# Fourier mixing and a gated convolution on one core: the odd columns of the odd samples computed as a DCT-IV

## The chip, the cores and the metric

The kernel runs on one core of one Trainium2 chip. A core has TensorE (PE, matmuls; its weight loads, PEld, are listed apart), VectorE (DVE), ScalarE (ACT), GpSimd (POOL) and SyncE (SP, which issues DMAs). The metric is the device time of one execution in microseconds (us); lower is better.

## The reference

Input x has 8 batches of 3136 x 256 numbers (float32). The first part is the real part of a two-dimensional Fourier transform of each batch; the second is a feed-forward layer whose hidden values are gated by a sigmoid of a convolution over the sequence with three taps.

```python
X = np.fft.fft(np.fft.fft(x, axis=1), axis=2).real       # per batch: sequence, then features
h = np.maximum(X @ w_in, 0.0)                             # 256 -> 1024
conv = sum(conv_w[k] * h_padded[:, k:k + S, :] for k in range(3))
out = (h * sigmoid(conv)) @ w_out                         # 1024 -> 256
```

The weights arrive as float64 and are narrowed to float32 in the kernel by integer operations on VectorE.

## The kernel before

The transform along the sequence uses the symmetries of cosine and sine. For each batch, `fold_ops` adds and subtracts rows of x and their mirror images on VectorE until a quarter of the sequence is left, and writes the result as the tile `w`: two of them, one for even and one for odd frequencies (`wt[b][0]`, `wt[b][1]`), each with 98 or 99 partitions, four parts, four groups of samples q and 128 features. A batch has two halves of the fold (`half(h)`), each an ordered list of seven operations, most of them an instruction of 1000 elements per partition or two of 500: `pair(0)`, `pair(2)`, `both(6)`, `feats(1)` (which writes the odd `w`), `both(4)`, `evens`, `feats(0)`. Beside them `single`, a small copy on GpSimd, fills the first column of each part of `w`.

`units` then multiplies `w` by tables of cosines and sines that a DMA has loaded into SBUF. There are eight units a batch (the ninth, `feature`, exists for batch 0 alone): for each of sn = 1 and 0 (sine and cosine) `odd_even`, `odd`, `even_even` and `even`. A unit is a few matmuls into one PSUM tile, then a copy of a part of it to SBUF on ScalarE (`copy`), then additions and subtractions on VectorE (`fin`). `odd` has four matmuls of HO = 392 columns, no copy, and two VectorE instructions of 392 elements that write the odd columns of `PQ` and their mirror image. One float32 matmul of the program appears in the profile as two instructions, each with a weight load. `tabs[0]` holds the even tables (two kinds, four sample groups, 393 columns), `tabs[1]` the odd ones (four kinds: two are loaded, and `mirror_tables` makes the other two on ScalarE).

The rest of the work is a list of 256 steps: 8 batches x 4 chunks of columns x 8 blocks of 128 hidden features. A step's parts are spread over several turns (cycles) of the last loop of the program. In cycle t:

- TensorE does `products` of step t+1 (`pb`, `pa`: two matmuls of some 387 columns, the second part of the transform and `w_in` in one) and then `mm2` of step t-3 (`po`, six matmuls of 256 columns with `w_out`);
- ScalarE does `sigmoid` of step t-2, `copies` of step t+1 (out of `pb`), `seed` of step t+2, `first_tap` of step t;
- VectorE does `combine` of step t (L719), `tap` 1 of step t-1 (L730), then what is hung into the cycle under the name "dve" (a fold operation or the `fin` of a unit), `tap` 2 of step t-1, and `gate` of step t-2 (L754);
- GpSimd does its share of the gate (L753) and issues the indirect loads of x.

Each engine works in the order of the program. Folds and units of later batches are hung into these cycles by hand: `ends` lists in which cycle the fold of each batch must be over (9, 20, 44, 68, 96, 125, 157, 189), and the units of that batch run from there to three cycles before its first step. `at(cycle, where, fn)` hangs an operation into a cycle: "act" stands after `copies` on ScalarE, "dve" between the two taps on VectorE, "pe" after `mm2` on TensorE. A cycle that is in `taken` gets no fold operation.

Batch 0 runs before the steps. VectorE folds both halves (from 8.7 us), then narrows the first quarter of `w_in`. TensorE meanwhile runs 16 instructions without use to keep its clock up (`keep_on`, which read the odd `w` of the first half), and then the parts of the four odd units in turn (`u.part(i)`). The tables are loaded on SP's queue behind the loads of x; the odd tables first, then a quarter of `w_in`, then the even ones.

Of the kernel before, what the change touches and what calls it, by code (L numbers as in the profile page):

```python
# [30 lines left out]
NQ = 8  # L31
# [5 lines left out]
def kernel(  # L37
# [103 lines left out]
    def fold_ops(b):  # L141
# [4 lines left out]
        def half(h):  # L146
# [60 lines left out]
        (o0, s0), (o1, s1) = half(0), half(1)  # L207
        return o0 + o1, {**s0, **{len(o0) + j: f for j, f in s1.items()}}

    tabs = [const.tile([P, n, HQ, HE], F32, name="tab%d" % n) for n in (2, 4)]
# [3 lines left out]
    def table(k, st, q, cols):  # L216
        return tabs[st // 2][0:k, st, q, cols] if st < 2 else tabs[1][0:k, st - 2, q, cols]

    def load_tables(par):


        st = slice(2 * par, 2 * par + 2)
        to = tabs[par][:, 0:2].rearrange("p s q i -> p s (q i)")
        n = HQ * HE
        m = NP // 2 // 16 * 16
        for i in range(2):
            nc.sync.dma_start(out=to[i:2 * m:2], in_=dft_seq[0:m, st, HQ * i:HQ * (i + 1)]
                              .rearrange("p s q i -> p s (q i)"))
        assert NP == 2 * m + 2
        nc.sync.dma_start(out=to[2 * m:NP], in_=bass.AP(  # L230
            tensor=dft_seq.tensor, offset=dft_seq.offset + (m * 4 + 2 * par) * NQ * HE,
            ap=[[n, 2], [NQ * HE, 2], [1, n]]))
        nc.sync.dma_start(out=to[NP:KR], in_=bass.AP(
            tensor=dft_seq.tensor, offset=dft_seq.offset + ((NP * 4 + 2 * par) * NQ - HQ + 2) * HE,
            ap=[[n, 1], [NQ * HE, 2], [1, n]]))

    def mend_row(par, half):

        for st in range(2):
            row = tabs[par][96:NP, st, HQ - 1]  # L240
            act(row, row, AF.Copy, scale=half[96:NP])

    def mirror_tables(q):

        for to, of, s in ((2, 1, -1.0), (3, 0, 1.0)):
            for i in range(2):
                act(tabs[1][0:KR, to, q:q + 2, i:HO:2], tabs[1][0:KR, of, q:q + 2, i:HO:2], AF.Copy,
                    scale=-s if i else s)
# [31 lines left out]
    def units(b):  # L280
# [52 lines left out]
        def odd(sn):  # L333
            prods = [(q, wf, st) for q in (0, 2) for wf, st in stat(sn)]
            mms = [product((slice(0, P), slice(0, HO)), wf, st, q, slice(0, HO), i == 0, i == 3)
                   for i, (q, wf, st) in enumerate(prods)]

            def fin(p):
                a, bb, t = a_[sn][:, 0:HO], p[:, 0:HO], PQ[b][sn]
                vt(t[:, 1:Q4 + 1:2], a, bb, op=ALU.add)  # L340
                x0, x1 = (bb, a) if sn else (a, bb)
                vt(t[:, M - 1:Q4:-2], x0, x1, op=ALU.subtract)
            return Unit(b, mms, lambda p: None, fin)
# [277 lines left out]

    nc.gpsimd.memset(tabs[1][0:1, 0, 0, 0:1], 0.0)
    load_tables(1)
    w_in[0].load(nc.sync)
    load_tables(0)
# [172 lines left out]
    for f in fold_ops(0)[0]:  # L798
        f()
# [6 lines left out]
    mirror_tables(0)  # L806
    mend_row(1, half)
    mirror_tables(2)
# [61 lines left out]
    ends = [9, 20, per + 12] + [per * (b - 1) - 3 + max(11 - 4 * (b - 2), 0) for b in range(3, B)]  # L870
# [37 lines left out]
    for b in range(1, B):  # L908
        ops, singles = fold_ops(b)
        c0, n = ends[b - 1], ends[b] - ends[b - 1]  # L910
        if b == 1:

            cs = [c for c in range(4, ends[1] + 1) if c not in taken]
            assert len(cs) == len(ops) and cs[7] > NF + 4
# [3 lines left out]
        if b + 1 < B:  # L918
            for h in range(2):
                for j, fn in enumerate(load_ops(b + 1, h, nc.sync)):  # L920
                    at(cs[7 * h + 6] + 1 + j, "load", fn)
# [112 lines left out]
```

## Time and profile before

| | |
|---|---|
| time, median of 3 runs | 1188.49 us (1187.96 to 1189.62) |
| span of the profiled execution (first to last instruction) | 1184.7 us; its whole time is not listed, and the runs lie 3.3 to 4.9 us above this span |
| PE busy | 1158.7 us (98%) |
| DVE busy | 1128.7 us (95%) |
| ACT busy | 886.7 us (75%) |
| POOL busy | 407.6 us (34%) |
| mean granted clock of TensorE | 0.998 |

A line of the timeline gives the start, the length, the engine, the line of the code, the instruction, what it writes and reads, its shape and how many of its kind follow each other; in brackets stand the idle time of the engine before it and what ended it. Lengths overlap: an instruction often starts before the one ahead of it on the same engine has ended, so what an engine can do in a time is read from start to start (the pitch). Groups of instructions give count, busy time in us and mean length in ns. Windows give the busy time of PE, PEld, DVE, ACT and POOL in a stretch.

### The profile page before, as it was taken

The page shows a single profiled execution, that of the slowest core. Times are in us where ns is not written, and L with a number is a line of the kernel's source. Part 1 is how long each engine was busy: PE and PEld are TensorE (multiplying, and loading weights), DVE is VectorE, ACT ScalarE, POOL GpSimd, SP SyncE. Part 2 cuts the span into 40 slices and gives each one's busy share as a digit, 9 for nine tenths or more (in the row PEclk, how much of TensorE's full clock was granted, in tenths as well). Part 3 has the DMA queues.
Part 4 walks back from the last instruction along what each step waited for, and adds up shares of the span by engine and source line. Part 5 has one row for each costly group of instructions (what it writes and reads, how often), then busy time and mean ns, then how long its engine had stood idle before and what let it go on. Part 6 is the DMA issues. An engine that isn't in the chain of part 4 may idle for free.

```text
span 1184.7 us, 15354 instructions
## 1 busy us (share of the span) xinstructions
PE 1158.7 (98%) x4820; PEld 891.6 (75%) x4820; DVE 1128.7 (95%) x1633; ACT 886.7 (75%) x1888; POOL 407.6 (34%) x476
## 2 busy tenths in 40 slices
PE   4999999999999999999999999999999999999998
PEld 2667777777777777777777777777777777777776
DVE  7899999999999999999998999999998898999996
ACT  2578668777777778877777877877777777888885
POOL 5225443433434342424333232432322232222222
PEclk9999999999999999999999999999999999999999
DMA  9803233121212021202131110310010100100000
GB/s 226 195 10 107 57 55 89 49 69 41 72 38 86 28 77 52 83 7 76 34 96 46 48 48 14 104 34 27 27 34 21 32 27 27 51 31 27 28 27 32
DMA packets 70068, 66.08 MB, mean 56 GB/s; under 512 B 28107, under 2 KB 57683, under 8 KB 69987
## 3 DMA queue, kind: packets, MB, share of 16 engines
q1 hardware_dynamic: 64349, 51.98, 15.6%
q0 software_dynamic: 5120, 12.85, 3.7%
q8 instruction: 38, 0.62, 0.2%
q14 instruction: 43, 0.35, 0.1%
q10 hardware_dynamic: 518, 0.28, 0.1%
HBM read 39.33 MB, written 25.74 MB: 55 GB/s over the span
## 4 chain that ended last, share of the span: by engine, by line
PE 89%; DVE 7%; issue 1%; POOL 1%; ACT 1%; DMA 0%; DVEq 0%; SPq 0%; POOLq 0%; ACTq 0%
PE po L92 54%; PE pb L92 14%; PE pa L92 13%; PE pd L92 8%; DVE g L730 3%; DVE h L719 1%; DVE g L754 1%; POOL xh L131 1%; DVE raw L558 0%; DVE xh L167 0%; DVE wout L551 0%; ACT os L778 0%; DVE w L194 0%; DVE win L551 0%; DMA out_dram<-os 0%
## 5 line engine op out<-in xcount | busy, mean ns | idle before, releaser
L92 PE MATMUL po<-wout,g 128*128 128x256 f32 x3072 | 706.1, 379 | 4.2 <-DVE g L754 4.2
L92 PEld LDWEIGHTS po<-wout,g 128*128 128x128 f32 x3072 | 580.8, 190 | 148.7 <-issue 20.0
L730 DVE SCALAR_TENSOR_TENSOR g<-h,cw,g 128x770 f32<-128x770 f32 (+1 forms) x512 | 575.7, 1124 | 5.7 <-ACT g L725 2.1
L753 POOL TENSOR_TENSOR g<-g,h 128x385 f32<-128x385 f32 (+2 forms) x256 | 270.4, 1057 | 721.1 <-ACT g L745 542.1
L708 ACT ACTIVATE nb<-pb 128x386 f32<-128x386 f32 (+2 forms) x494 | 219.9, 500 | 168.2 <-PE pb L92 167.5
L745 ACT ACTIVATE g<-g 128x385 f32<-128x385 f32 (+4 forms) x512 | 244.8, 531 | 81.8 <-DVE g L730 78.4
L719 DVE CUSTOM_DVE_ANT_0 h<-pa,nb 128x386 f32<-128x386 f32 (+2 forms) x503 | 260.0, 556 | 2.5 <-POOL h L686 2.5
L725 ACT ACTIVATE g<-h,cw 128x770 f32<-128x770 f32 (+1 forms) x256 | 244.2, 954 | 0.0
L92 PE MATMUL pb<-qt,G 127*128 127x387 f32 (+2 forms) x512 | 213.7, 498 | 0.9 <-ACT G L641 0.9
L92 PE MATMUL pa<-pt,G 128*128 128x387 f32 (+2 forms) x512 | 211.8, 494 | 0.0
L672 ACT ACTIVATE pa<-eb,ge 128x387 f32<-128x387 f32 (+2 forms) x256 | 155.2, 607 | 0.6 <-ACT ft L477 0.6
L92 PEld LDWEIGHTS pa<-pt,G 128*128 128x128 f32 x512 | 96.9, 189 | 73.5 <-issue 18.0
L754 DVE TENSOR_TENSOR g<-g,h 128x385 f32<-128x385 f32 (+2 forms) x256 | 147.7, 577 | 2.4 <-ACT g L745 2.4
L92 PE MATMUL pd<-tab,w 98*128 98x196 f32 (+3 forms) x448 | 115.9, 356 | 0.0
L92 PEld LDWEIGHTS pb<-qt,G 127*128 127x128 f32 x512 | 91.5, 190 | 18.8 <-ACT G L641 1.9
L131 POOL DMA_INDIRECT xh<-in_x_dram,idx x64 | 99.8, 1560 | 13.0 <-issue 10.6
L92 PEld LDWEIGHTS pd<-tab,w 98*128 98x128 f32 (+1 forms) x448 | 82.7, 191 | 12.6
L778 ACT COPY os<-po 128x256 f32<-128x256 f32 x196 | 57.6, 397 | 6.6 <-PE po L92 3.3
L156 DVE TENSOR_TENSOR xh<-xh 98x1020 f32<-98x1020 f32 (+1 forms) x32 | 40.4, 1265 | 2.6 <-DMA xh<-in_x_dram,idx 2.6
L167 DVE TENSOR_TENSOR xh<-xh 98x1024 f32<-98x1024 f32 (+1 forms) x32 | 40.5, 1266 | 0.1
L178 POOL COPY w<-xh 98x4 f32<-98x4 f32 (+1 forms) x32 | 24.2, 758 | 6.1 <-DVE xh L167 3.6
L193 DVE TENSOR_TENSOR w<-xh 98x508 f32<-98x508 f32 (+1 forms) x32 | 23.0, 720 | 0.1
(124 smaller groups left out, 330.3 us busy)
## 6 DMA issues: line engine op xcount, KB each, us to landing
out_dram<-os SPq DMA_DIRECT2D x192, 128.0 KB
xh<-in_x_dram SPq DMA_DIRECT2D x16, 784.0 KB
eb<-ed SPq DMA_DIRECT2D x16, 193.5 KB
tab<-dft_seq_dram SPq DMA_DIRECT2D x4, 589.5 KB
raw<-in_moe_w_in_dram SPq DMA_DIRECT2D x4, 512.0 KB
raw<-in_moe_w_out_dram SPq DMA_DIRECT2D x1, 2048.0 KB
eb<-ed SPq DMA_DIRECT2D x8, 209.0 KB
eb<-ed SPq DMA_DIRECT2D x7, 193.0 KB
```

The source lines that it names most:

```text
L92: nc.tensor.matmul(o, l, r, start=start, stop=stop, skip_group_check=True)
L131: nc.gpsimd.indirect_dma_start(out=xh[b, h][0:NP, 7 - m].rearrange("p q d -> p (q d)"), out_offset=None, in_=bass.AP(tensor=x.tensor, offs ...
L167: vt(flat(to, to + 2), flat(0, 2), flat(2, 4), op=op)
L672: act(pa[s][:, 0:n], eb[b, c], AF.Copy, scale=ge[:, f:f + 1])
L708: act(nb[s][:, i, cols], p[:, cols], AF.Copy, scale=-1.0 if i else 1.0)
L719: nc.vector._custom_dve(TENSOR_ADD_SAT, out=to, in0=a[:, cols], in1=c[:, i, cols], s0=BIG, s1=0.0)
L725: act(gs[s], hs[s][:, 0:n], AF.Copy, scale=cw[:, 0, s[2]:s[2] + 1])
L730: stt(out=g, in0=h[:, k:k + n], scalar=cw[:, k, f:f + 1], in1=g, op0=ALU.mult, op1=ALU.add)
L745: act(gs[s][:, c], gs[s][:, c], AF.Sigmoid)
L753: gt(g[:, p], g[:, p], h[:, p], op=ALU.mult)
L754: vt(g[:, v], g[:, v], h[:, v], op=ALU.mult)
L778: nc.scalar.copy(out=osb[:, j % 2], in_=pt[:, j % 2])
```

## The change

The odd samples (groups q = 0 and 2) at the odd frequencies form a transform in which both indices are odd (a DCT-IV, and the sine of the same kind). The new kernel turns each pair of values by an angle that depends on the sample alone, and can then use the even tables, at every second column, 197 instead of 392, for two of the turned parts in place of the odd tables; sums and differences of the two results give all odd columns. In detail:

- Fold: behind `both(4)` each half gets an eighth operation, `turned`: two `scalar_tensor_tensor` of 98 x 256 on VectorE, in place in the odd `w`. Ahead of it, in the same cycle under "act", `scaled` writes two products of 98 x 256 on ScalarE into a new tile `rt`. The angles are the tile `turn`, loaded by four DMAs of 98 single numbers each on ScalarE's queue at the start.
- `odd`: four matmuls of 197 columns in place of 392, a copy of 197 columns on ScalarE, and two more VectorE instructions of 196 elements ahead of the two of 392, whose operands are now both in SBUF.
- Tables: of the odd ones two sample groups and 196 columns are left. Eight small DMAs load them, then the even ones follow, and `w_in` behind both. The mirroring shrinks from eight instructions of 392 elements to four of 196.
- The fold of batch 1 must be over in cycle 22 instead of 20, so its units start two cycles later.

```diff
@@ fold_ops @@
-            ops = [pair(0), pair(2), both(6, ALU.subtract), feats(1), both(4, ALU.add), evens, feats(0)]
-            return ops, {3: single(1), 6: single(0)}
+            def sides():
+                w = wt[b][1][0:NP, :, 2 * h]
+                return w[:, 0:4:2], w[:, 1:4:2]
+            made = []
+            def scaled():
+                made.append(rp.tile([P, 2, 2, P], F32, name="rt", tag="rt"))
+                for i, v in enumerate(sides()):
+                    act(made[0][0:NP, i], v, AF.Copy, scale=turn[0:NP, 1, h:h + 1])
+            def turned():
+                for i, v in enumerate(sides()):
+                    stt(out=v, in0=v, scalar=turn[0:NP, 0, h:h + 1], in1=made[0][0:NP, 1 - i],
+                        op0=ALU.mult, op1=ALU.add if i else ALU.subtract)
+            ops = [pair(0), pair(2), both(6, ALU.subtract), feats(1), both(4, ALU.add), turned, evens, feats(0)]
+            return ops, {3: single(1), 7: single(0)}, {5: scaled}
...
+    def load_turn(eng):
+        for s in range(2):
+            for i in range(2):
+                eng.dma_start(out=turn[i:NP:2, s].unsqueeze(2), in_=bass.AP(
+                    tensor=dft_seq.tensor, offset=dft_seq.offset + ((2 + s) * NQ + HQ * i) * HE,
+                    ap=[[4 * NQ * HE, NP // 2], [2 * HE, 2], [1, 1]]))
...
@@ units: odd(sn) @@
-            prods = [(q, wf, st) for q in (0, 2) for wf, st in stat(sn)]
-            mms = [product((slice(0, P), slice(0, HO)), wf, st, q, slice(0, HO), i == 0, i == 3)
-                   for i, (q, wf, st) in enumerate(prods)]
+            n = HE // 2 + 1
+            mms = [product((slice(0, P), slice(i * n, (i + 1) * n)), w(4 + 2 * sn + (i ^ sn)), i, q,
+                           slice(0, HE, 2), i == 0 and q == 0, q == 2)
+                   for q in (0, 2) for i in range(2)]
+            def copy(p):
+                a_["s", sn], a_["b", sn] = [asp.tile([P, HO + 2], F32, name="as", tag="as") for _ in range(2)]
+                nc.scalar.copy(out=a_["s", sn][:, 0:n], in_=p[:, n:2 * n])
             def fin(p):
-                a, bb, t = a_[sn][:, 0:HO], p[:, 0:HO], PQ[b][sn]
+                a, t = a_[sn][:, 0:HO], PQ[b][sn]
+                u, v, bb = p[:, 0:n], a_["s", sn][:, 0:n], a_["b", sn][:, 0:HO]
+                if sn:
+                    vt(bb[:, 0:HO:2], v[:, 0:n - 1], u[:, 0:n - 1], op=ALU.add)
+                    vt(bb[:, 1:HO:2], v[:, 1:n], u[:, 1:n], op=ALU.subtract)
+                else:
+                    vt(bb[:, 0:HO:2], u[:, 0:n - 1], v[:, 0:n - 1], op=ALU.subtract)
+                    vt(bb[:, 1:HO:2], u[:, 1:n], v[:, 1:n], op=ALU.add)
                 vt(t[:, 1:Q4 + 1:2], a, bb, op=ALU.add)
                 x0, x1 = (bb, a) if sn else (a, bb)
                 vt(t[:, M - 1:Q4:-2], x0, x1, op=ALU.subtract)
-            return Unit(b, mms, lambda p: None, fin)
+            return Unit(b, mms, copy, fin)
...
@@ start @@
+    load_turn(nc.scalar)
     nc.gpsimd.memset(tabs[1][0:1, 0, 0, 0:1], 0.0)
-    load_tables(1)
+    load_odd(nc.sync)
+    load_even()
     w_in[0].load(nc.sync)
-    load_tables(0)
...
@@ order of the side work @@
-    ends = [9, 20, per + 12] + [per * (b - 1) - 3 + max(11 - 4 * (b - 2), 0) for b in range(3, B)]
+    ends = [9, 22, per + 12] + [per * (b - 1) - 3 + max(11 - 4 * (b - 2), 0) for b in range(3, B)]
...
+        for j, fn in pres.items():
+            at(cs[j], "act", fn)
```

More of the change, by code (lines that the diff above doesn't have):

```diff
@@ L237, in mend_row @@
+    def load_turn(eng):
+        for s in range(2):
+            for i in range(2):
+                eng.dma_start(out=turn[i:NP:2, s].unsqueeze(2), in_=bass.AP(
+                    tensor=dft_seq.tensor, offset=dft_seq.offset + ((2 + s) * NQ + HQ * i) * HE,
+                    ap=[[4 * NQ * HE, NP // 2], [2 * HE, 2], [1, 1]]))
     def mend_row(par, half):
         for st in range(2):
-            row = tabs[par][96:NP, st, HQ - 1]
+            row = tabs[0][96:NP, st, HQ - 1] if par == 0 else tabs[1][96:NP, st, 1]
@@ L797 @@
     nc.gpsimd.memset(PQ[0][1][96:P, :], 0.0)
-    for f in fold_ops(0)[0]:
+    ops, _, pres = fold_ops(0)
+    for j, f in enumerate(ops):
+        if j in pres:
+            pres[j]()
         f()
```

54 lines of the change are left out of this document (34 added, 20 removed).

## The prediction

> **What bounds the kernel now.** I read the busy times, then the chain of waits, then a quiet cycle of the timeline, then windows.
>
> ```profile
> PE 1158.7 (98%) x4820; PEld 891.6 (75%) x4820; DVE 1128.7 (95%) x1633; ACT 886.7 (75%) x1888; POOL 407.6 (34%) x476
> ...
> PE 89%; DVE 7%; issue 1%; POOL 1%; ACT 1%; DMA 0%; DVEq 0%; SPq 0%; POOLq 0%; ACTq 0%
> ```
>
> By the shares both TensorE and VectorE look full; the chain that ended last is 89% TensorE. A quiet cycle late in the run (nothing hung in) tells them apart:
>
> ```profile
> 1067.35 0.87 POOL L753 TENSOR_TENSOR g<-g,h 128x385 f32<-128x385 f32 x1 [2.98 <-ACT g L745]
> 1067.51 2.57 DVE L730 SCALAR_TENSOR_TENSOR g<-h,cw,g 128x770 f32<-128x770 f32 x2
> 1067.69 0.81 PE L92 MATMUL pb<-qt,G 127*128 127x386 f32 x2
> 1068.34 0.81 PE L92 MATMUL pa<-pt,G 128*128 128x386 f32 x2
> 1068.54 0.87 ACT L708 ACTIVATE nb<-pb 128x385 f32<-128x385 f32 x2 [0.86 <-PE pb L92]
> 1068.99 2.75 PE L92 MATMUL po<-wout,g 128*128 128x256 f32 x12
> 1070.00 0.55 DVE L754 TENSOR_TENSOR g<-g,h 128x385 f32<-128x385 f32 x1
> 1071.58 0.82 PE L92 MATMUL pb<-qt,G 127*128 127x387 f32 x2
> ```
>
> TensorE's matmuls follow each other without a gap: 3.89 us from `pb` to `pb` (1067.69 to 1071.58), 2.59 of it for twelve `po`. ScalarE waits 0.86 us for it. VectorE's two taps take 2.49 us (1067.51 to 1070.00) while GpSimd's gate runs inside them. In another cycle the same instructions need less:
>
> ```profile
> 951.06 2.06 DVE L730 SCALAR_TENSOR_TENSOR g<-h,cw,g 128x770 f32<-128x770 f32 x2
> 953.04 0.56 DVE L754 TENSOR_TENSOR g<-g,h 128x385 f32<-128x385 f32 x1
> 953.51 1.02 DVE L719 CUSTOM_DVE_ANT_0 h<-pa,nb 128x386 f32<-128x386 f32 x2
> 954.45 1.01 DVE L730 SCALAR_TENSOR_TENSOR g<-h,cw,g 128x770 f32<-128x770 f32 x1
> ```
>
> From tap to tap: 3.39 us, the taps 1.98. So VectorE's own work in a cycle is 0.50 us below TensorE's, and the busy share hides it: it is stretched when it is early. TensorE is the bound where this holds, and VectorE where it does not:
>
> ```profile
> 80.00:100.00 20.00, 19.09 (x76) 13.95 (x75) 19.93 (x27) 14.46 (x29) 9.79 (x9) 1.00 0.17 51
> 200.00:250.00 50.00, 49.40 (x205) 36.67 (x205) 49.32 (x73) 39.57 (x88) 21.28 (x27) 1.00 0.16 50
> 550.00:600.00 50.00, 50.00 (x209) 38.39 (x208) 49.03 (x74) 38.13 (x78) 19.00 (x18) 1.00 0.10 31
> ...
> PEld po L92 <- DVE g L754: 15.6, 24, 1.5
> 220.27 2.86 PE L92 MATMUL po<-wout,g 128*128 128x256 f32 x12 [0.37 <-DVE g L754]
> ```
>
> Up to some 120 us, and again around 200 to 260 us, TensorE loses time to VectorE's gate (windows of 19.09 of 20 and 49.40 of 50; the wait of 0.37 at 220.27); from 550 on it loses none.
>
> **TensorE's gain.** In batch 1 whole units stand in one cycle:
>
> ```profile
> 141.04 2.80 PE L92 MATMUL pd<-tab,w 98*128 98x392 f32 x8
> 143.68 0.81 PE L92 MATMUL pb<-qt,G 127*128 127x387 f32 x2
> 156.38 1.56 PE L92 MATMUL pd<-tab,w 98*128 98x197 f32 x8
> 157.78 0.87 PE L92 MATMUL pb<-qt,G 127*128 127x418 f32 x2
> 25.72 8.10 PE L92 MATMUL po<-tab,w 98*128 98x196 f32 x32
> ```
>
> Eight instructions of 392 columns take 2.64 us (0.33 each), eight of 197 from the same strided even table 1.40 (0.175). An odd unit saves 1.24; with two a batch that is 2.48, and 17.4 for batches 1 to 7. In batch 0 the 16 of 392 among the 32 at 25.72 save 2.5. The new form is in the trace, so this term is nearly certain as work.
>
> **VectorE's cost.** The rows nearest to each added instruction:
>
> ```profile
> 948.18 0.36 DVE L298 TENSOR_TENSOR as<-as,pd 128x197 f32<-128x197 f32 x1 [1.99 <-ACT as L294]
> 948.45 0.36 DVE L300 TENSOR_TENSOR as<-pd,as 128x196 f32<-128x196 f32 x1
> 948.73 1.01 DVE L730 SCALAR_TENSOR_TENSOR g<-h,cw,g 128x770 f32<-128x770 f32 x1
> 930.33 0.55 DVE L340 TENSOR_TENSOR qt<-as,pd 128x392 f32<-128x392 f32 x1
> 930.80 0.55 DVE L342 TENSOR_TENSOR qt<-pd,as 128x392 f32<-128x392 f32 x1
> L558 DVE SCALAR_TENSOR_TENSOR raw<-raw 128x512 f32<-128x512 uint32 x3 | 2.1, 693 | 0.1
> L641 ACT COPY G<-po 128x256 f32<-128x256 f32 x8 | 2.7, 372 | 3.3 <-PE po L92 3.3
> ```
>
> An odd `fin` gets two additions of 196, 0.27 us each by pitch, and a wait of 0.1 for their result (taps that depend on each other take 1.98 where two single ones would take 1.87, estimated from the lengths): 0.65 a unit, 1.3 a batch. `turned` is four instructions of 256 elements a batch. They lie between 0.27 (the 196 above) and 0.61 (0.69 long for 512, less the 0.08 by which lengths overlap); I take 0.33, as 256 is much nearer to 196: 1.3 a batch. Together 2.6; by the ends 2.4 and 3.7. ScalarE gets four products of 256 (0.37 at most each, by L641) and two copies of 197, some 2.1 a batch; it is busy 75% and waits for `pb` in every quiet cycle, so I cost it at nothing except where VectorE waits for it.
>
> Does VectorE have 2.6 us? In a batch the quiet cycles leave 32 x 0.50 = 16; the units add some 12.4 of TensorE (16 x 0.33, and 48 of the smaller forms at 0.10 to 0.175), folds and `fin`s some 22.4 of VectorE (a fold operation of 1000 elements has a pitch of 1.14, an estimate from a length of 1.2; eight such, four of 0.6, eight of 0.6; `fin`s of 6.0, eight instructions of 0.27 and eight of 0.47). That leaves 6, some 8 with the longer last chunks, in which TensorE has more room still. The change takes 2.6 on one side and 2.5 on the other, so about 3 remain: TensorE stays first over a batch, with VectorE ahead in more places.
>
> The row at 948.18 shows a new kind of wait: VectorE stood 1.99 us until ScalarE had copied a part of the product. `odd` had no copy; now it has, and `turned` waits for `scaled` in the same way, four such places a batch. Behind each in VectorE's queue stand tap 2 and the gate that `po` needs. In a cycle that begins with `pb` at 0, ScalarE starts `copies` at 0.85 (1067.69 to 1068.54), ends them at 1.64 and the new copy near 2.0; the longer `fin` ends at 3.6, tap 2 at 4.55, the gate at 5.1. The next `po` starts at 3.89 + 1.30 = 5.2, later where a unit's matmuls lie between (0.3 to 0.6). It fits, barely: I take 0 and keep 0.5 for each of 28 as the other end.
>
> [...]
>
> [...]
>
> **The start.** In front of the first step VectorE, GpSimd and TensorE hang together:
>
> ```profile
> 13.66 1.22 DVE L167 TENSOR_TENSOR xh<-xh 98x1024 f32<-98x1024 f32 x1
> 14.91 0.69 DVE L171 TENSOR_TENSOR xh<-xh 98x512 f32<-98x512 f32 x1
> 15.63 0.64 POOL L199 TENSOR_TENSOR w<-xh,sg 98x4 f32<-98x4 f32 x1
> 15.71 4.64 PE L92 MATMUL pb<-w 98*128 98x512 f32 x5 [8.87 <-POOL w L178]
> 29.44 0.69 DVE L561 SCALAR_TENSOR_TENSOR win<-raw,win 128x512 f32<-128x512 f32 x1
> 32.55 0.36 DVE L328 TENSOR_TENSOR as<-as,po 128x196 f32<-128x196 f32 x1 [2.42 <-ACT as L324]
> 45.52 11.67 SPq L436 DMA_DIRECT2D ft<-in_x_dram  x3
> ```
>
> `turned` stands where L171 started at 14.91. It needs `scaled`, and that needs the columns that GpSimd writes until 16.27 (15.63 + 0.64): two products make it 17.0. VectorE stands 2.1 us, then works 0.7; the second half costs 0.7 without a stall. `keep_on` reads the turned `w`, so TensorE's row at 15.71 moves to about 17.7, and the odd parts from 25.72 to 27.7; with the 2.5 saved they end no later. VectorE is 3.5 late at 30.1; the 2.42 us it waited before 32.55 absorb that much; the longer `fin`s add 1.3, a shorter wait later gives back 0.4: some +2.0. Up to 120 us VectorE sets the pace, so this reaches the steps.
>
> The DMAs: `turn` has 392 single numbers. The three gathers at 45.52 (3136 numbers each) hold their queue 3.9 us each, so by that rate these take 0.5; between that and four plain issues they are there long before 16.3, and loads of the odd tables, though eight, carry a quarter of the bytes. ScalarE's queue holds nothing urgent then. The first quarter of `w_in` now lands behind the even tables (by the tiles' sizes 1.2 MB of even tables more ahead of it, and 0.9 MB of odd ones less), and VectorE asks for it 3.5 us later too. `scaled` of the second half stands ahead of the mirroring on ScalarE, to some 26 us; the mirrored tables are first read by the second round of odd parts, at some 29, and mirroring has shrunk to a quarter. I cost all this at 0; if one landed only at 20 us, 3 us more.
>
> **Up to 260 us.** To the 2.0 VectorE adds batch 1's turn (1.3) and `fin`s (1.3) and batch 2's turn (1.3): 5.9 by the end of the second fold, where it sets the pace. Batch 1's units also stand closer (9 cycles instead of 11). Against it stand VectorE's idle time (0.7 in 200:250, some 2.5 over 120 to 260 us) and stretched taps, perhaps 1: I take +2.5 at 260 us, and batch 1's saving of 2.48 is gone in it. Ends: 0 and +6.
>
> **The sum.** From batch 2 on six batches save 2.48 each: -14.9. In the stretches between the units of one batch and the next, where only folds run, VectorE is ahead for a few cycles; that costs +1.5 in all (0 to 4). -14.9 + 2.5 + 1.5 = -10.9. The span goes from 1184.7 to 1174; the runs lie 3.8 above it at the median, so 1188.5 becomes 1177.6; I say 1178.
>
> **Rivals.**
> - All of the saving comes through: the start is absorbed and VectorE follows, -17.4 and 0 for the start: 1171. For it: the new matmul form is in the trace and 550:600 has no gap. Against it: the waits at 220.27 and before.
> - VectorE is the bound at its busy share. 49.03 of 50 leaves 1 us in 50, 2.8 in a batch, if the stretch is not elastic but belongs to the work. Then 2.6 of new work uses it up, a batch takes what it took, and the start (+2.0 to +2.5) remains: 1191. It decides from 2.8 us of added VectorE time a batch, which any contention with GpSimd passes. Against it: the cycle at 951.06, and that a quiet cycle shows VectorE full with 3.39 of work.
> - The new waits for ScalarE's copies reach `po`: 0.2 us for 28 of them, 5.6 more than I forecast: 1183 to 1184.
> - The change does not do what it says, if matmuls of 197 were paced by their weight loads; the row at 156.38 (0.175) excludes it.
>
> **Chances.** The forecast (1174 to 1181) 0.45; all comes through 0.15; ScalarE's waits 0.20; VectorE the bound, or something like it in the start, 0.20. Changes within 0.2% (2.4 us) can hardly be measured. Faster: the first three, 0.78 with a little taken off the third; same 0.05; slower 0.17. The range, 1171 to 1191, leaves out the tails of the first and last cases.
>
> **What would show it.** Right: 16-instruction groups of 98x197 at 0.175 in the `pd` rows, TensorE without gaps from 300 us on, quiet-fold stretches with waits of `po` for the gate, PE busy some 18 to 20 us less, DVE busy up at most by a few, first steps some 2 us later. Wrong: waits of `po` on the gate in the 550:600 window, DVE at 50 of 50 with unstretched taps, or a first `po` much later than 63 us.

## The result and the profile after

The changed kernel takes 1195.62 us (median of four runs, 1194.77 to 1195.90) against 1188.22 us (1185.01 to 1189.62) for the kernel before on the same chip: ratio 1.0067, 95% interval 1.0053 to 1.0081. It is slower by 0.7%; I had said 1178. The span of the profiled execution went from 1184.7 to 1193.9 us.

The busy times and the shares of the chain of waits, after:

```profile
PE 1154.3 (97%) x4820; PEld 891.5 (75%) x4820; DVE 1135.4 (95%) x1697; ACT 898.3 (75%) x1932; POOL 403.3 (34%) x476
...
PE 74%; DVE 16%; issue 4%; ACT 3%; DMA 2%; POOL 1%; SPq 0%; DVEq 0%; POOLq 0%; ACTq 0%
```

TensorE is busy only 4.4 us less (1158.7 to 1154.3) where the change takes some 20 us of matmuls away (in e7_matmuls below, without VectorE's added work, it is 18.4 less: 1140.3); VectorE has 6.7 us more. On the chain TensorE's share fell from 89% to 74% and VectorE's rose from 7% to 16%. The same windows as before (columns: window, length, then busy time and count of PE, PEld, DVE, ACT, POOL, then granted clock, DMA share, GB/s), and a stretch around 365 us:

```profile
80.00:100.00 20.00, 18.25 (x71) 12.94 (x70) 19.86 (x31) 13.13 (x27) 5.11 (x13) 1.00 0.12 31
200.00:250.00 50.00, 48.06 (x196) 34.60 (x195) 49.15 (x73) 37.66 (x82) 20.78 (x27) 1.00 0.20 57
340.00:390.00 50.00, 48.49 (x194) 35.39 (x193) 48.88 (x73) 37.10 (x82) 21.16 (x27) 1.00 0.22 64
550.00:600.00 50.00, 49.78 (x215) 39.52 (x214) 49.76 (x76) 38.34 (x79) 23.85 (x20) 1.00 0.19 59
```

The waits after (what waits, for what; us in all, times, longest):

```profile
PEld po L92 <- DVE g L811: 48.5, 83, 1.8
...
PE po L92 <- DVE g L811: 10.2, 22, 1.2
```

TensorE is short of full in all four (before: 19.09 of 20, 49.40 of 50, 49.97 in 340:390 and 50.00 in 550:600), and its waits for the gate, 15.6 and 4.2 us before, are 48.5 and 10.2 (most of the first kind is a weight load that waits beside a running matmul). VectorE's new waits for ScalarE, in the groups of waits after (L217 is `turned`, L391 and L394 the first addition of an odd `fin`):

```profile
DVE w L217 <- ACT rt L213: 6.5, 12, 2.0
...
DVE as L394 <- ACT as L385: 3.1, 3, 1.7
...
DVE as L391 <- ACT as L385: 2.0, 4, 0.8
```

To see where the time went, I compare the start of each step's `po` matmuls in the two traces (worked out from the TensorE rows; step 41 starts at 252.3 us before, which ends the stretch that the prediction called "up to 260 us"):

| stretch | predicted | measured |
|---|---|---|
| start of the program to the first `po` (63.0 us before, 72.7 after) | +2.0 | +9.7 |
| first `po` to step 41 | +0.5 | +5.9 |
| step 41 to the last step | -13.4 | -6.5 |
| sum | -10.9 | +9.1 |

Differences in the text are taken before rounding. The profiled execution of the kernel before, which all of them are measured against, was itself a quick one: in every run listed core by core the time is some 1.8 us above the span, which would make it some 1186.5 us, 1.7 under the median. So +9.1 by the traces is +7.4 by the medians.

The loss has three places of some 5 to 8 us each. The start, after; SyncE's queue of DMA issues first, then VectorE, ScalarE and TensorE (brackets: idle time before, and what ended it):

```profile
13.86 1.38 SPq L264 DMA_DIRECT2D tab<-dft_seq_dram  x2
...
20.39 1.26 SPq L249 DMA_DIRECT2D tab<-dft_seq_dram  x2
...
22.85 0.43 SPq L633 DMA_DIRECT2D raw<-in_moe_w_in_dram  x1
```

```profile
31.09 0.43 DVE L599 TENSOR_SCALAR win<-raw 128x512 int32<-128x512 int32 x1 [1.39 <-DMA raw<-in_moe_w_in_dram]
...
35.00 0.35 DVE L371 TENSOR_TENSOR as<-as,po 128x196 f32<-128x196 f32 x1
```

```profile
35.73 0.32 ACT L367 COPY as<-po 128x196 f32<-128x196 f32 x1 [1.00 <-DVE as L373]
37.33 0.33 ACT L385 COPY as<-po 128x197 f32<-128x197 f32 x1 [1.27 <-DVE qt L398]
37.67 1.13 ACT L284 ACTIVATE tab<-tab,half 2x393 f32<-2x393 f32 x2
```

```profile
29.68 5.38 PE L92 MATMUL po<-tab,w 98*128 98x197 f32 x30 [0.92 <-DMA tab<-dft_seq_dram]
38.39 1.48 PE L92 MATMUL pd<-tab,ea 99*1 99x197 f32 x16 [3.33 <-issue]
39.80 9.03 PE L92 MATMUL po<-tab,w 99*128 99x99 f32 x32
```

The two rows of the kernel before that answer to these, SyncE's first weight load and TensorE's 32 matmuls of 99 columns:

```profile
16.07 0.42 SPq L577 DMA_DIRECT2D raw<-in_moe_w_in_dram  x1
```

```profile
35.06 4.85 PE L92 MATMUL po<-tab,w 99*128 99x99 f32 x32
```

The eight small loads of the odd tables hold SyncE's queue from 13.86 to 20.39 (1.1 us of it is a wait for one of the table loads), and the first quarter of `w_in` is issued at 22.85 instead of 16.07. VectorE waits 1.39 us for it and reaches the first `fin` at 35.00. Behind each `fin` stands a copy of ScalarE that needs its tile, and behind those copies, at 37.67, `mend_row` of the even tables (L284). The feature unit reads what it writes: TensorE stands 3.33 us and starts at 38.39. Then its clock is at half; the 32 matmuls of 99 columns take 9.03 us instead of 4.85. The stretch behind the gap, after and then before:

```profile
38.50:55.50 17.00, 17.00 (x66) 13.55 (x58) 11.87 (x25) 4.15 (x11) 6.63 (x12) 0.50 0.79 242
```

```profile
38.50:55.50 17.00, 15.56 (x62) 11.14 (x62) 16.45 (x32) 9.21 (x22) 5.39 (x9) 0.90 0.92 230
```

The granted clock is 0.50 for 17 us, though TensorE is busy all the time by the row; VectorE, busy 16.45 of the 17 us before and 11.87 now, waits for what TensorE makes (the longest wait there, 1.95 us, is for ScalarE's copy of a `po` tile).

### The profile page after: what moved, and what is told of

The parts are those of the page before. It is cut to its first block, busy times and chain, and to the rows that moved or that the text cites. A ratio compares the mean times of both kernels' runs of the same rounds, so it can differ in the third digit from the quotient of the medians.

```text
span 1193.9 us, 15499 instructions
## 1 busy us (share of the span) xinstructions
PE 1154.3 (97%) x4820; PEld 891.5 (75%) x4820; DVE 1135.4 (95%) x1697; ACT 898.3 (75%) x1932; POOL 403.3 (34%) x476
## 4 chain that ended last, share of the span: by engine, by line
PE 74%; DVE 16%; issue 4%; ACT 3%; DMA 2%; POOL 1%; SPq 0%; DVEq 0%; POOLq 0%; ACTq 0%
PE po L92 47%; PE pb L92 11%; PE pa L92 11%; DVE g L787 7%; PE pd L92 5%; DVE h L776 3%; DVE g L811 2%; POOL xh L131 1%; DMA tab<-dft_seq_dram 1%; ACT nb L765 1%; DVE w L194 1%; ACT g L802 0%; DMA xh<-in_x_dram 0%; ACT rt L213 0%; ACT os L835 0%
## 5 line engine op out<-in xcount | busy, mean ns | idle before, releaser
L92 PE MATMUL po<-wout,g 128*128 128x256 f32 x3072 | 709.8, 381 | 10.8 <-DVE g L811 10.2
L92 PEld LDWEIGHTS po<-wout,g 128*128 128x128 f32 x3072 | 577.6, 190 | 166.3 <-DVE g L811 48.5
L787 DVE SCALAR_TENSOR_TENSOR g<-h,cw,g 128x770 f32<-128x770 f32 (+1 forms) x512 | 564.9, 1103 | 4.1 <-ACT g L782 0.9
L810 POOL TENSOR_TENSOR g<-g,h 128x385 f32<-128x385 f32 (+2 forms) x256 | 264.5, 1034 | 729.3 <-ACT g L802 549.4
L131 POOL DMA_INDIRECT xh<-in_x_dram,idx x64 | 102.3, 1598 | 13.0 <-issue 9.7
L92 PE MATMUL pd<-tab,w 98*128 98x197 f32 (+2 forms) x448 | 98.5, 318 | 1.0 <-DVE w L194 1.0
L213 ACT ACTIVATE rt<-w,turn 98x256 f32<-98x256 f32 x32 | 14.5, 508 | 14.7 <-POOL w L199 14.7
```

The lines of the kernel that those rows point to most:

```text
L92: nc.tensor.matmul(o, l, r, start=start, stop=stop, skip_group_check=True)
L131: nc.gpsimd.indirect_dma_start(out=xh[b, h][0:NP, 7 - m].rearrange("p q d -> p (q d)"), out_offset=None, in_=bass.AP(tensor=x.tensor, offs ...
L787: stt(out=g, in0=h[:, k:k + n], scalar=cw[:, k, f:f + 1], in1=g, op0=ALU.mult, op1=ALU.add)
L810: gt(g[:, p], g[:, p], h[:, p], op=ALU.mult)
```

## Experiments

My theory after reading the traces was this: the start is lost to the order of ScalarE's queue (and the clock that falls with TensorE's gap), the steady part to VectorE's waits for ScalarE's copies, and the rest to VectorE's added work. The rivals: the late loads alone; contention between the engines; ScalarE's load. All times are medians; each ratio is against runs of the kernel before that were taken with it. "Step 0", "step 41" and "end" are the starts of those `po` against the kernel before, from the traces.

| run | time, us | ratio (95% interval) | step 0 | step 41 | end |
|---|---|---|---|---|---|
| changed kernel | 1195.62 | 1.0067 (1.0053 to 1.0081) | +9.7 | +15.6 | +9.1 |
| e1_mend | 1189.11 | 1.0008 (0.9998 to 1.0018) | +4.6 | +10.3 | +3.8 |
| e2b_fill | 1190.92 | 1.0030 (1.0012 to 1.0047) | +2.5 | +8.2 | +2.9 |
| e5_loads | 1193.80 | 1.0052 (1.0035 to 1.0069) | +8.6 | +14.5 | +7.4 |
| e3_first | 1189.70 | 1.0018 (1.0008 to 1.0028) | +8.7 | +12.7 | +2.9 |
| e4_both | 1183.99 | 0.9965 (0.9953 to 0.9978) | +3.3 | +7.3 | -2.6 |
| e6_three | 1183.72 | 0.9967 (0.9956 to 0.9979) | +2.5 | +6.5 | -3.3 |
| e7_matmuls | 1175.96 | 0.9910 (0.9893 to 0.9926) | +2.4 | +3.1 | -11.6 |
| e8_noturn | 1177.27 | 0.9910 (0.9895 to 0.9925) | +6.0 | +7.8 | -6.4 |
| e9_noadd | 1182.81 | 0.9964 (0.9950 to 0.9978) | +2.3 | +4.9 | -5.6 |
| e13_noscale | 1179.85 | 0.9936 (0.9924 to 0.9949) | +4.0 | +5.1 | -5.5 |
| e12_pace | 1181.11 | 0.9952 (0.9940 to 0.9964) | +2.1 | +6.1 | -5.5 |

The first `po` varies though the start is the same: it stands at 65.2 to 69.0 us in the profiles of e4, e7, e8, e9 and e13. For the latest, e8_noturn, the trace shows why: its granted clock is at 0.50 from 28.9 to 35.7 us, where the other four have 1.00. So the steady part is best read from one step to another, not from the total, and from step 41 on best of all: e13_noscale starts 1.7 us later than e9_noadd and is 0.2 behind it at step 41.

### The start: the order of ScalarE's queue

```diff
@@ e1_mend: start of batch 0 @@
     mirror_tables()
+    mend_row(0, half)
     for i in range(4):
...
-    mend_row(0, half)
```

> The scaling of the even tables' last row (mend_row of the even tables) goes on ScalarE ahead of the odd units' copies in place of behind them; nothing else moves. Theory 1 (ScalarE's order opens the gap of 3.33 us that TensorE has before the feature unit, and the gap lets the granted clock fall): the gap falls under 1 us, the clock does not stay at 0.5 from 38 to 55 us, the first po starts some 5 to 7 us earlier than its 72.7 (66 to 68), the time falls by as much, to 1188.5 to 1190.5. Rival 2 (the gap is from elsewhere, the late weights or VectorE): the start and the time stay, 1195.6. Rival 3 (the gap goes, but the clock falls all the same, for the work itself is thin there): 2 to 3 us, 1193.

The first `po` came at 67.6 instead of 72.7 and the time fell to 1189.11, both as theory 1 said. TensorE in e1_mend:

```profile
29.95 5.38 PE L92 MATMUL po<-tab,w 98*128 98x197 f32 x30 [1.39 <-DMA tab<-dft_seq_dram]
35.26 0.88 PE L92 MATMUL pd<-tab,ea 99*1 99x197 f32 x16
36.07 4.85 PE L92 MATMUL po<-tab,w 99*128 99x99 f32 x32
```

The odd parts end as late as in the changed kernel, but the feature unit follows without a gap, and the 32 matmuls take 4.85 us again. The clock still falls, but later and for less: it is at 0.50 from 44.9 to 51.8 us, behind a gap of 1.80. One `mend_row` in the wrong place of ScalarE's queue cost 6.5 us (5.3 by the last `po` of the two traces). To part the gap from the clock, the next kernel left ScalarE's order alone and gave TensorE something to do:

```diff
@@ e2b_fill: start of batch 0 (e2_keep: eight banks instead of four) @@
+    keep_on([idle] * 4)
     mend_row(0, half)
```

> ScalarE's order stays as in the changed kernel; eight matmuls of 512 columns whose result nobody reads fill TensorE's gap before the feature unit (about 3.4 us at full clock). Theory 1 (an idle TensorE costs the clock): the feature unit starts as late as before (38.4), but the clock stays at 1.0, the even units' 32 matmuls take 5 us in place of 9, the first po is 4 to 5 us earlier, the time 1190.5 to 1192. Rival (the clock falls for another reason, or VectorE sets the start whatever the clock): the time stays or grows by up to 1, 1195.6 to 1196.6.

> The filling matmuls again, now half as many instructions: the first run issued sixteen instructions (7.0 us), twice the gap, so that it delayed the feature unit by 5 us and still brought the first po 1.0 us forward. With eight (about 3.5 us) the feature unit should start as in the changed kernel, near 38.4. Theory (an idle TensorE costs the clock): no stretch of 0.5 from 38 to 55 us, first po 4 to 5 us earlier than 72.7, time 1190.5 to 1192. Rival (VectorE sets the start, whatever the clock): first po as in the first run, 71.7, time 1194 to 1195.

The first of the two was badly sized: each bank takes two instructions, so sixteen ran, 7.0 us, and pushed the feature unit to 43.38. Even so its first `po` was 1.0 us earlier than the changed kernel's, and the time 1193.66. With half of it, TensorE in e2b_fill:

```profile
33.46 3.59 PE L92 MATMUL pb<-w 98*128 98x512 f32 x8
36.98 0.88 PE L92 MATMUL pd<-tab,ea 99*1 99x197 f32 x16
37.79 4.85 PE L92 MATMUL po<-tab,w 99*128 99x99 f32 x32
```

The feature unit starts 1.4 us earlier (the wait for the even tables did not occur in this profile), and the 32 matmuls run at full clock. The clock is at 0.50 for 3.4 us (from 44.9) instead of 17. The first `po` is 7.2 us earlier, so most of the 5 to 7 us is the clock, not the gap of 3.33 us itself. In the total 4.7 are left: TensorE gives 1.2 back in one stall at step 129 that the changed kernel doesn't have, and whose cause I did not find. The loads alone were the rival:

```diff
@@ e5_loads: start of batch 0 @@
-    nc.gpsimd.memset(tabs[1][0:1, 0, 0, 0:1], 0.0)
-    load_odd(nc.sync)
+    nc.gpsimd.memset(tabs[0][0:1, 0, 0, 0:1], 0.0)
     load_even()
     w_in[0].load(nc.sync)
+    load_odd(nc.sync)
```

> The changed kernel with only the order of loads altered: the even tables (with the wait for GpSimd that stood ahead of the odd ones) and the first quarter of the weights are issued ahead of the eight small loads of the odd tables, which occupy SP's queue from 13.9 to 20.4 us while little moves. Theory (those eight issues are what makes the weights late, and with them VectorE, ScalarE's copies, the row's scaling and the clock): VectorE's wait of 1.4 us for the weights and TensorE's of 0.9 for the even tables go, TensorE's gap of 3.3 us shrinks to 1.5 or less, the first po comes 3 to 7 us earlier (66 to 70), time 1189 to 1192.5. Rival (the odd tables then land too late for mirroring and the first parts): the start stays or gets worse, 1195 to 1199.

This missed. TensorE and ScalarE in e5_loads:

```profile
36.41 1.49 PE L92 MATMUL pd<-tab,ea 99*1 99x197 f32 x16 [3.74 <-ACT tab L284]
37.83 9.02 PE L92 MATMUL po<-tab,w 99*128 99x99 f32 x32
```

```profile
35.30 0.33 ACT L385 COPY as<-po 128x197 f32<-128x197 f32 x1 [1.27 <-DVE qt L398]
35.66 1.13 ACT L284 ACTIVATE tab<-tab,half 2x393 f32<-2x393 f32 x2
```

Both waits for loads are gone and everything is 2 us earlier, but the gap stays (3.74, now put down to L284 by name), the clock falls all the same, and 1.1 us is left of it at the first `po`. The late loads were a cost, but not the cause. Nor are the eight loads all that makes the weights late: in e5_loads they stand behind the weights, which are issued at 19.70 all the same (22.85 in the changed kernel, 16.07 before), because SyncE's queue waits there for a table load:

```profile
SPq L633 <- DMA tab<-dft_seq_dram: 3.8, 1, 3.8
```

### The steady part: waits for ScalarE, and VectorE's work

```diff
@@ e3_first: units and folds of batches 1 to 7 (early is set for the odd units) @@
-            at(cs[i + 1], "act", u.copy)
+            at(cs[i + 1], "first" if u.early else "act", u.copy)
...
-            at(cs[j], "act", fn)
+            at(cs[j], "first", fn)
```

> From batch 1 on the odd units' copies and the products for the turn go on ScalarE ahead of the copies of the next step's products in place of behind them, so that VectorE should find them done. Theory (VectorE's waits for these copies reach TensorE, as the third rival of the prediction said): VectorE's waits for ScalarE's rt and as go, TensorE's waits for the gate fall by 3 to 5 us, the time is 1190.5 to 1192.5. Rival (VectorE's added work itself is the price, the waits cost nothing): 1194.6 to 1196.

> Both of the above moves on ScalarE, without the filling matmuls. If the two losses are separate, their gains add up: 1184 to 1187 by the first theory of each, which is faster than the kernel before; 1188.5 to 1190.5 if only the start was lost to ScalarE's order; 1195.6 if neither was.

e3_first took 1189.70 us. VectorE's waits for `rt` and the odd copies, 11.6 us in the changed kernel, are 2.1 (most of it in batch 0), and TensorE's for the gate fell from 48.5 and 10.2 to:

```profile
PEld po L92 <- DVE g L812: 36.5, 64, 1.6
...
PE po L92 <- DVE g L812: 7.6, 16, 1.0
...
DVE w L217 <- ACT rt L213: 1.8, 2, 1.5
```

From the first `po` to step 41 the kernel gains 1.9 us on the changed one (+4.0 instead of +5.9), from there to the end 3.3 (-9.8 instead of -6.5). In e4_both the two moves add up: 1183.99 us, 11.6 less than the changed kernel, and now faster than the kernel before. The loads on top of it (e6_three) brought nothing that the times can tell from e4_both:

> The two moves on ScalarE together (1184.0) and the altered order of loads as well. Theory: the first po goes from 66.3 to some 64 to 65 (VectorE's wait of 1.4 and TensorE's of 2.4 are gone, what stays is the turn and the longer fins), the time 1182 to 1183. Rival (odd tables late): 1184 to 1188.

What is VectorE's work worth? The next three leave work out on top of e4_both, in batches 1 to 7 (e7 and e8 also end the folds of batch 1 in cycle 20 again):

```diff
@@ e8_noturn: fold_ops (e7_matmuls has both edits) @@
+            if b:
+                del ops[5]
+                return ops, {3: single(1), 6: single(0)}, {}
@@ e9_noadd: odd(sn) @@
+                if b == 0:
                     nc.scalar.copy(out=a_["s", sn][:, 0:n], in_=p[:, n:2 * n])
...
+                if b:
+                    bb = p[:, 0:HO]
```

> On top of the two moves on ScalarE, batches 1 to 7 do the new matmuls alone: the turn (products and the four VectorE instructions, with the old pace of batch 1's folds) and the odd units' copies and additions are left out, the two instructions of 392 read the product from PSUM as before; the output is not the reference's. Theory (TensorE's saving is 2.48 a batch, VectorE's added work eats the rest of it): from the first po (66.3) on all of the 17.4 us comes through, time 1188.2 + 3.3 - 17.4 = 1174. Rival (something else, such as the units that stand closer or the shorter cover for ScalarE, takes a part): 1177 to 1181.

> The kernel with the two moves on ScalarE, without the turn in batches 1 to 7 (products and the four VectorE instructions left out, the old pace of batch 1's folds; the odd units' copies and additions stay): the output is not the reference's. The matmuls alone reached 1176 against 1184 with everything, so VectorE's added work costs 8.0 us in all. Theory by amount of VectorE work (the turn has 1.6 us a batch by pitch, the additions 1.3): 1179.5 to 1180. Theory by place (the additions make a cycle long in which a unit's fin already stands, the turn stands alone in its cycle): 1181.5 to 1183.

> The same kernel without the odd units' copies and additions in batches 1 to 7 (their two instructions of 392 read the product from PSUM as before; the turn stays): the output is not the reference's. By amount: 1180 to 1180.5. By place: 1177 to 1178.5.

With the matmuls alone TensorE's gain is there: from step 41 to the end -14.7 us, six batches of 2.45 (predicted 2.48). Up to step 41 it is +0.7: as predicted, batch 1's saving does not come through where VectorE sets the pace (the 1174 of the expectation had counted it). The window at 365 us, e7_matmuls:

```profile
340.00:390.00 50.00, 49.97 (x210) 39.04 (x209) 49.86 (x73) 38.20 (x83) 18.21 (x26) 1.00 0.18 52
```

TensorE is full there; in the changed kernel it had 48.49. All of the added work of VectorE, with ScalarE's for it, costs 8.0 us (1175.96 against 1183.99). But it does not go by amount. Neither theory had it right: the turn costs 6.1 to 6.6 us from the first `po` on (e9 against e7, e4 against e8), the additions 1.6 to 2.1; from step 41 on, where the late start of e8 plays no part, 4.2 to 4.4 and 0.5 to 0.7. Yet by the rows below the turn needs 1.6 us a batch (two instructions in 0.79), and the additions 1.3 (in e4_both 0.65 a unit, from the first addition at 791.24 to the first instruction of 392 at 791.89).

My reading is that it matters where they stand. I counted in each trace the cycles in which VectorE has nothing but the step's own work between its two taps:

| cycles | before | e7, e8 (no turn) | e4, e9, changed kernel | e12_pace |
|---|---|---|---|---|
| 22 to 43 | 5 of 22 | 5 of 22 | 3 of 22 | 3 of 22 |
| 44 to 67 | 2 of 24 | 2 of 24 | 0 of 24 | 4 of 24 |
| 68 to 95 | 6 of 28 | 6 of 28 | 4 of 28 | 6 of 28 |
| 96 to 124 | 8 of 29 | 8 of 29 | 6 of 29 | 7 of 29 |

The turn is an operation of its own in the list of folds, and each one takes a cycle that was empty. The additions stand in cycles that were full already. In cycles 57 to 71 of e4_both and e12_pace (a run further down) an empty one takes VectorE 3.4 to 3.8 us from gate to gate, a full one 4.0 to 5.8, and TensorE without its losses 3.8 to 5.1, by how many matmuls of units stand in it: VectorE catches up mostly in the empty ones. A part of cycles 63 to 65 in e4_both, where none is left, with the gate (L812) that `po` waits for:

```profile
350.29 0.54 DVE L812 TENSOR_TENSOR g<-g,h 128x384 f32<-128x384 f32 x1
...
352.83 1.21 DVE L167 TENSOR_TENSOR xh<-xh 99x1024 f32<-99x1024 f32 x1
353.97 1.07 DVE L788 SCALAR_TENSOR_TENSOR g<-h,cw,g 128x832 f32<-128x832 f32 x1
354.96 0.55 DVE L812 TENSOR_TENSOR g<-g,h 128x384 f32<-128x384 f32 x1
...
357.45 0.87 DVE L217 SCALAR_TENSOR_TENSOR w<-w,turn,rt 98x256 f32<-98x256 f32 x2
358.24 1.01 DVE L788 SCALAR_TENSOR_TENSOR g<-h,cw,g 128x770 f32<-128x770 f32 x1
359.17 0.55 DVE L812 TENSOR_TENSOR g<-g,h 128x384 f32<-128x384 f32 x1
```

From gate to gate 4.67 and 4.21 us, with no empty one from step 57 to step 67. To test this I moved the folds apart, with nothing left out (the units of a batch follow its folds, so those of batches 3 to 7 are moved too and get 17 cycles):

```diff
@@ e12_pace, on top of e6_three @@
-    ends = [9, 22, per + 12] + [per * (b - 1) - 3 + max(11 - 4 * (b - 2), 0) for b in range(3, B)]
+    ends = [9, 22, per + 12] + [per * (b - 1) - 3 + 15 for b in range(3, B)]
```

> Nothing left out: the two moves on ScalarE, the altered loads (1183.7), and the folds of batches 3 to 7 end 15 cycles into the next 32 for every batch in place of 11, 7, 3, 0 and 0 (so cycles 76, 108, 140, 172 and 204 in place of 72, 100, 128, 157 and 189; each batch's units get 17 cycles). Theory by density (the turn takes the cycles without a side operation in which VectorE caught up; TensorE's loss of 6.2 us from step 41 on stands in the dense cycles around steps 61 to 67 and 91 to 95): the losses at steps 61 to 67 shrink to 1 us or less, those at 91 to 95 too, the time 1180 to 1181.5. Rival (the turn costs by contention or through ScalarE wherever it stands): 1183 to 1185.

(The old ends in that text are wrong: they are 68, 96, 125, 157 and 189, as the list of the kernel before has them, from extras of 7, 3, 0, 0 and 0. The new ones are right. TensorE's losses in it are sums of what lies between the starts of two matmuls beyond 0.842 ns a column (2.64 us for eight of 392 columns, from 141.04 us on in the kernel before), where that is above 0.06 us.) It took 1181.11 us, as expected, but only half of the expected came true. The losses at steps 61 to 67, 2.8 us in e6_three, are 0.2. Those at 91 to 98 stay at 2.1, though cycles 68 to 95 have 6 empty ones again, as in the kernel before, which loses 0.9 there. And new ones come at steps 155 to 162: 2.1 us, 0.6 in e6_three. With the units moved away TensorE's cycles there (158 to 165) take 3.8 to 4.0 us without losses, 4.1 to 4.3 in e6_three, so it asks more of VectorE; that this is the reason was not tested. The count of empty cycles in a stretch alone does not tell the loss. From step 41 on the kernel gains 11.6 us on the one before, e6_three 9.8. The same stretch of VectorE in e12_pace:

```profile
352.10 0.54 DVE L812 TENSOR_TENSOR g<-g,h 128x384 f32<-128x384 f32 x1
...
353.50 2.21 DVE L788 SCALAR_TENSOR_TENSOR g<-h,cw,g 128x770 f32<-128x770 f32 x2
355.64 0.55 DVE L812 TENSOR_TENSOR g<-g,h 128x384 f32<-128x384 f32 x1
```

An empty cycle, both taps in one row, 3.54 us from gate to gate, and in the window TensorE is full:

```profile
340.00:390.00 50.00, 50.00 (x206) 38.81 (x205) 49.26 (x73) 41.14 (x89) 18.00 (x27) 1.00 0.11 35
```

Two controls, e13_noscale (VectorE's four instructions in place, ScalarE's products gone; on top of e9_noadd) and the new pace in the kernel before:

```diff
@@ e13_noscale: fold_ops, batches 1 to 7 @@
+                if b == 0:
                     for i, v in enumerate(sides()):
                         act(made[0][0:NP, i], v, AF.Copy, scale=turn[0:NP, 1, h:h + 1])
...
+                    if b:
+                        stt(out=made[0][0:NP, i], in0=v, scalar=turn[0:NP, 0, h:h + 1], in1=v,
+                            op0=ALU.mult, op1=ALU.add)
+                        continue
```

> The kernel without the odd units' copies and additions (1182.8), and in batches 1 to 7 ScalarE's products for the turn are left out too, while VectorE still does four instructions of 98x256 in the same place, on other data and into an unused tile: the output is not the reference's. Theory by density (VectorE's time in those cycles is the whole price of the turn): the same losses at steps 61 to 67 and 91 to 95, time 1181.5 to 1183. Rival (ScalarE's four products are the price): 1176 to 1178, as with the matmuls alone.

> The kernel before, with the new pace of the folds alone. It loses only 1.4 us to VectorE from step 41 on, so there is nothing to win: 1186.5 to 1189. If it gains as much as the changed kernel does by the pace, the pace is not an answer to the change but a gain of its own.

The time of e13_noscale, 1179.85, lies between the two expectations, but its trace is clear: TensorE loses at the same steps and by as much as in e9_noadd (1.12 us ahead of step 66, and 10.5 gained from step 41 to the end, in both). So from step 41 on ScalarE's products are not the price. The medians differ by 3.0 us, 1179.85 against 1182.81, where the two profiled executions, which took 1181.12 and 1180.92, agree; whether the products cost something in batch 1 stays open. The kernel before with the new pace takes 1188.28 us, ratio 1.0008 (0.9999 to 1.0017): nothing to win there. So what the pace wins it wins against the turn.

Three more had no effect that the times can tell. The two instructions of 392 put into a later cycle than the additions, so that no cycle holds all four:

```diff
@@ e10_split, on top of e6_three (e14_best: on top of e12_pace) @@
+            if u.late:
+                at(min(cs[i + 1] + 3, cs[i + 2] - 1), "dve", lambda u=u: u.late(u.p))
```

> Nothing left out: the two moves on ScalarE and the altered loads, and from batch 2 on the odd unit's two instructions of 392 stand in a later cycle (up to three later) than its additions, so that no cycle holds all four. Theory by place: 1.5 to 3.5 us less than the 1183.7 without the split, 1180 to 1182. Theory by amount: 1183 to 1184.5.

> Nothing left out: the new pace together with the split of the odd unit's fin. If density is the cause, 1179 to 1181; if the pace does nothing, 1182 to 1183 as with the split alone.

They took 1182.31 (ratio 0.9957, 0.9943 to 0.9970) and 1181.45 us (0.9950, 0.9938 to 0.9963), within the intervals of e6_three and e12_pace; from step 41 to the end e10_split gains 10.1 us against e6_three's 9.8. Yet it uses up 8 of the 89 empty cycles of e6_three, one of them in cycles 68 to 95 and one in 96 to 124: an empty cycle that takes work over from a full one costs nothing here. And the additions written into PSUM, so that the instructions of 392 again read one operand from there:

```diff
@@ e11_psum: odd(sn), fin, on top of e6_three @@
+                to0, to1 = p[:, 0:n - 1], p[:, n + 1:2 * n]
...
+                    vt(to1, u[:, 1:n], v[:, 1:n], op=ALU.add)
+                    vt(to0, u[:, 0:n - 1], v[:, 0:n - 1], op=ALU.subtract)
```

> Nothing left out: the two moves on ScalarE and the altered loads, and the odd unit's additions write their result into the product's own PSUM bank, so that the two instructions of 392 again have one input in PSUM and one in SBUF, as in the kernel before. [...]

1183.87 us, 0.9969 (0.9958 to 0.9979): no difference from e6_three. So whether these two instructions read one operand from PSUM or both from SBUF has no price here that the times can tell. Nor had GpSimd an occasion to stretch the added work: by the rows of the changed kernel none of its 32 instructions of `turned` (0.47 to 0.49 us each) and none of its 32 of 392 (0.56 to 0.59) overlaps an addition or copy of GpSimd. In e6_three two of `turned` do, and one of the two took 1.03 us instead of 0.48 (GpSimd's row, then VectorE's pair, in which the first is the long one):

```profile
468.89 1.85 POOL L811 TENSOR_TENSOR g<-g,h 128x448 f32<-128x448 f32 x1 [4.46 <-ACT g L803]
...
469.99 1.43 DVE L217 SCALAR_TENSOR_TENSOR w<-w,turn,rt 98x256 f32<-98x256 f32 x2
```

So contention of GpSimd with the added instructions is not what the change lost to.

## Why the prediction was wrong, point by point

- **TensorE's gain, 2.48 a batch.** Right: 2.45 in e7_matmuls.
- **Start, +2.0; wrong, +9.7.** The failed step is "ScalarE's queue holds nothing urgent then", and with it "I cost all this at 0". The queue holds the `mend_row` that the feature unit needs, behind copies that now wait for later `fin`s. It opened a gap of 3.33 us and let the clock fall to half for 17 us; e1_mend gives back 6.5 us. The second failed step put the loads at 0 because they carry a quarter of the bytes: SyncE's queue was held for 6.5 us by the eight, and two waits (1.39 and 0.92) are gone in e5_loads, where the eight stand last. I had listed every instruction that moved, but counted SyncE's in bytes and not in issues, and did not ask what stands behind ScalarE's new copies. With both mended the first `po` stands 1.7 to 2.7 us later than before in five profiles, which is what the rest of that step had worked out.
- **VectorE's cost, 2.6 a batch.** The size was nearly right: 2.9, of it 1.6 for `turned` (0.40 each by pitch, I took 0.33) and 1.3 for the additions.
- **"Does VectorE have 2.6 us?"** Wrong. The sum of 6 to 8 us is a mean over a batch, while the slack is used cycle by cycle. The dense stretches had 2 empty cycles in 24 and 6 in 28, and the turn takes 2 of them a batch. VectorE's added work cost 4.9 us from step 41 on (e7_matmuls -14.7, e4_both -9.8) where I had put 1.5, and 3.3 up to step 41 (+4.0 against +0.7) where I had put 0.5. These sizes are measured; that it goes by the place of the turn is shown in part (steps 61 to 67 in e12_pace).
- **ScalarE's waits, "It fits, barely: I take 0".** Wrong. The moves of e3_first won 1.9 and 3.3 us, 5.2 in all; the third rival said 5.6. The margin of 0.1 us between gate and `po` was worked out for a cycle that starts on time; that the dense cycles start late and have none is my reading.
- **Up to step 41.** The direction was right (batch 1's saving is lost), the size not: ScalarE's waits 1.9 and VectorE's work 3.3 come on top.
- **Rivals.** The third and a part of the second (VectorE the bound, in places) came true together, and the start's loss was in none of them, but for the words "or something like it in the start" in the last chance, which had no mechanism. I had a rival for the new waits and one for VectorE, but each with the start of the forecast.

The terms add up: instead of -10.9, 7.7 more at the start, 5.2 for ScalarE's waits and 2.8 + 3.4 for VectorE's work make +8.2; measured +9.1. Of the rest, 0.7 is the stretch up to step 41 with the matmuls alone (+0.7, where batch 1's saving lost alone would be 0), and 0.2 the difference of 2.45 and 2.48.

The best version found is e12_pace, which does all of the change: 1181.11 us, 0.5% under the kernel before. Against the prediction's terms it lacks 3.5 us between the first `po` and step 41 (+4.0 where I had +0.5), where the folds of batches 1 and 2 leave 3 empty cycles in 22, and 1.8 from there on.

## What to carry to other kernels

When an engine that is 95% busy gets new work, don't ask how much slack a batch has, but in which cycles the work lands and how long the other engine's own cycle is there. Here 1.6 us a batch in cycles that had been empty cost 4.2 us or more from step 41 on, and 1.3 us in cycles that were full already 0.7 or less. For each instruction that an edit puts ahead of others on an in-order queue, name what stands behind it and who waits for that, also on the engine that looks idle (here one `mend_row` behind ScalarE's new copies cost 6.5 us); and count small DMAs by the time that they hold their queue, not by their bytes (here eight held SyncE's for 6.5 us).

## What was not expected of the hardware

- After a gap of 3.33 us TensorE's granted clock stayed at 0.50 for 17 us, with TensorE busy for 17.00 of them by its rows (in e5_loads for 20 us, after 3.74 us, with TensorE busy for 16.54 of the 17 us from 38.5 on). The gap does not tell here when the clock falls: in the changed kernel it fell as the gap ended (1.00 from 36.0 to 38.4 us, 0.55 from 38.4 to 39.0), in e5_loads 2.8 us after the gap began, and in the kernel before at 42.3 us, though no gap of TensorE in the eight us ahead of that is over 0.30. Nor do TensorE's busy rows tell when it comes back: in the kernel before the clock was at half for 3.4 us (0.51 from 42.3 to 45.7 us, with TensorE busy for 3.29 of them), in the changed one for 17. Whether the work behind the gap kept the clock down, matmuls of 99 columns and of one among them, was not tried.
- The eight loads of the odd tables, four of 73.5 KB and four of 1.5 or 3.1 KB by the trace's list of DMA issues, held SyncE's queue for 6.5 us, a wait of 1.1 among it, longer than the 3.1 us in which it issued the four larger ones and a weight load before.
